# Sums of x moved from the matrix to the vector engine, scan products held over one step, two turns replaced by a transposing load

## The chip, the cores and the metric

The kernel runs on one core of one Trainium2 chip. The metric is the device time of one execution in microseconds (us), the median of several. For the experiments, five timed runs of each kernel were made in turns with nine of the kernel before on the same chip. The profiled execution gives a span that is about 2 us shorter than the time.

PE is the matrix engine (TensorE), PEld its weight loads, DVE the vector engine, ACT the scalar engine, POOL GpSimd, SP the sync engine that issues most DMAs.

## The reference, cut to what matters

Two independent parts on different inputs, put side by side in the output:

```python
# part A: a diagonal complex state space layer, T = 2048 tokens, D = P = 1024
Bu = einsum('bld,pd->blp', x, B_bar)
h[t] = Lam_bar * h[t-1] + Bu[t]                 # the scan
y = 2 * Re(einsum('blp,dp->bld', h, Cmat)) + x * Dskip
# part B: attention in 64 segments of 32 tokens, each with 8 memory rows that the segment before wrote
h = concat([mem, x_segment]); q, k, v = h @ Wq, h @ Wk, h @ Wv      # 32 heads of 128
o = softmax(mask(q k^T)) v @ Wo;  mem = o[:8]
```

The kernel first computes part A's scan (stage 1) together with part B's values v = x Wv, then part A's output (stage 2), then part B's attention and output. It breaks the chain of memories by a guess: the memory of a segment is guessed from the mean of its tokens (`xbar`), later checked. So it needs the sum of x over each segment of 32 tokens: the "sums of x".

## The kernel before

Stage 1 works in 32 steps, 8 groups of states by 4 blocks of 512 tokens. PE makes `u` (psU, two buffers), DVE turns it by a table, scans it, and turns it back (the "products" `n`, `h`); ACT makes `g`, a bf16 copy of the scan, between the two.

```python
def stage1(self, pc, tb):
    u = k.ps("U", (128, 2, TB))                  # 16 matmuls of 512 columns
    ...
    V.tensor_tensor(pr[:], u[:]..., t3, ALU.mult)            # a_pr<-psU: frees psU
    w = pr[:, :, 0, :]
    V.tensor_tensor(w, w, pr[:, :, 1, :], ALU.add)
    for j in range(2):
        V.tensor_tensor_scan(w[:, j, :], rb, w[:, j, :], ini, ALU.mult, ALU.add)
        S.activation(g[:, j, :], w[:, j, :], ACT.Copy)       # a_g, on the scalar engine
    ...
    V.tensor_tensor(n[:], g[:]..., r3, ALU.mult)             # a_n: has to wait for a_g
    V.tensor_tensor(h[:], n[:, :, 0, :], n[:, :, 1, :], ALU.add)
    k.SP.dma_start(self.hs[tb][:, pc, :, :], h[:])
```

Between the steps PE makes blocks of four value tiles into psP (three buffers), which ACT empties into `b_vst` in its own order:

```python
def v_x(self, hb, q, w):
    ...                                          # cut: the first block, below
    for i in range(4):
        p = k.ps("P")[:]
        self.v_mm(p, w, 4 * q + i)               # 8 matmuls of 512 columns
        k.copy("s", st[:, i, :, 0:E], p)         # b_vst<-psP on the scalar engine
    Q.dma_start(vx[...], st[...])
```

The sums of x are matmuls with a matrix of ones and zeros, on row tiles loaded for them alone; two tiles, that is 16 matmuls of 4 columns, stand before each of the scan steps 3 to 10. The first four token tiles are turned on PE:

```python
def sum_x(self, tmp):                            # cut
    p = k.ps("R")
    for t in range(TT):
        for c in range(KC):
            k.PE.matmul(p[:, o:o + 4], xr[:, c * 128:(c + 1) * 128], k.ind[:], start=True, stop=True)
        load(t + 4)

def turn_x0(self, i):                            # 8 transposes on PE, a copy on DVE or ACT
    for c in range(KC):
        k.PE.transpose(pt[:, c, :], self.x0[i][:, c * 128:(c + 1) * 128], k.ident[:])
    k.copy("vs"[i % 2], self.xe[:, :, 128 * i:128 * i + 128], pt)
```

Every instruction that `k.PE` issues is recorded at one helper line, L68; every copy at L93 (ACT) or L95 (DVE). Groups are told apart by the names of what they write and read.

## Time and profile before

| | before |
|---|---|
| time, median of 4 runs | 1243.44 us (1243.30 to 1243.81) |
| span of the profiled execution | 1241.5 us |
| PE busy | 1230.8 us, 99% |
| DVE busy | 667.8 us, 54%; but 53.5 of the 60 us from 100 to 160 us |
| PE's waits, all | 2.9 us in four |

From the page of the kernel before: engine busy time with its share of the span and the number of instructions recorded, the granted PE clock in tenths over 40 slices, and the chain of waits by engine.

```profile
PE 1230.8 (99%) x8246; PEld 658.8 (53%) x8318; DVE 667.8 (54%) x1254; ACT 266.6 (21%) x695; POOL 278.1 (22%) x442
PEclk9999999999999999999999999999999999999999
PE 96%; DMA 3%; issue 0%; SPq 0%; DVE 0%
```

PE is the whole story: it never stops and its clock is full. (Matmuls are pipelined: one of 512 columns is recorded with 379 ns, but the next starts 216 ns later. A wait that the list puts at 0.94 us therefore delays PE by 163 ns more, from start to start.) This is the full list of PE's waits of the kernel before: who waited for whom, us in total, how many times, the longest.

```profile
PE psR L68 <- DVE hpb L109: 1.3, 1, 1.3
PE psO L68 <- DMA b_v<-b_vx: 0.9, 1, 0.9
PE psP L68 <- DMA b_wv<-in_B_Wv_dram: 0.4, 1, 0.4
PE psU L68 <- DMA b_xr<-in_B_x_dram: 0.3, 1, 0.3
```

The chain of waits of the kernel before in order of time (start, length, what, how many instructions). It holds the landing of the first weights (at 2.85 + 6.71 us), the first `u`, one of eight bunches of sums, and two of the "values of the guess" (32 matmuls into psR), one in mid-stage and one at the end of stage 1.

```profile
2.85 6.71 DMA b_wv<-in_B_Wv_dram
...
36.57 3.45 PE psU L68 x16
...
67.65 0.38 PE psR L68 x16
...
171.00 0.93 PE psR L68 x32
...
347.40 0.93 PE psR L68 x32
```

The timeline of DVE of the kernel before, in two scan steps (start, length, line, operation, and in brackets the idle time before it with its releaser).

```profile
109.86 2.27 DVE L275 TENSOR_TENSOR a_pr<-psU,a_tabf 128x2048 f32<-128x2048 f32 x1
112.04 1.21 DVE L294 TENSOR_TENSOR a_n<-a_g,a_tabh 128x2048 bf16<-128x2048 bf16 x1
...
114.91 2.45 DVE L283 TENSOR_TENSOR_SCAN a_pr<-a_rr,a_nx,a_pr 128x512 f32<-128x512 f32 x2
118.05 1.23 DVE L294 TENSOR_TENSOR a_n<-a_g,a_tabh 128x2048 bf16<-128x2048 bf16 x1 [0.70 <-ACT a_g L284]
```

Two orders are to be seen. The first `a_n` here belongs to the step before and stands after the next `a_pr<-psU`: it waits for nothing. The last one comes right after its own scan and waits 0.70 us for `a_g`. DVE's waits in stage 1 (60 to 345 us) of the kernel before:

```profile
DVE a_n L294 <- ACT a_g L284: 15.3, 22, 0.7
DVE a_pr L275 <- PE psU L68: 10.1, 7, 2.0
```

So DVE is close to full from 100 to 160 us (53.5 of 60 us busy) but never holds PE.

### The profile page before, as it was taken

Reading aid. Unit: us, or ns where it says so; the run is one execution under the profiler, and the core shown is the slowest. Engines: PE = TensorE matmul, PEld = TensorE weight load, DVE = VectorE, ACT = ScalarE, POOL = GpSimd, SP = SyncE. Lnnn points to the kernel's source line nnn. Section 1 sums busy time; section 2 is a strip of 40 time slices with the busy share of each in tenths; the row PEclk is TensorE's granted clock in tenths of the full one; section 3 lists DMA queues with packets and bytes.
Section 4 is the critical chain, followed back from the end, with each engine's and each line's share of the span. In section 5 each row is a group of like instructions: output and inputs, shape, how many; then the busy total and the mean of one; then the engine's idle time right before and its main releaser. Section 6 shows DMA issues by size and latency. Waiting matters only on the chain.

```text
span 1241.5 us, 20294 instructions
## 1 busy us (share of the span) xinstructions
PE 1230.8 (99%) x8246; PEld 658.8 (53%) x8318; DVE 667.8 (54%) x1254; ACT 266.6 (21%) x695; POOL 278.1 (22%) x442
## 2 busy tenths in 40 slices
PE   9999999999999999999999999999999999999998
PEld 4444444444455555556565656556565654445444
DVE  4688899998811124666666666666666641001000
ACT  5344344443310000111112121212111210000000
POOL 4111331222322330232223232222322220000000
PEclk9999999999999999999999999999999999999999
DMA  9965444644898834675464554545564279507000
GB/s 251 267 184 158 131 120 133 156 143 118 221 325 247 267 109 106 150 200 139 109 153 108 126 135 114 131 94 140 112 146 101 59 198 252 113 17 154 17 17 27
DMA packets 322357, 178.42 MB, mean 144 GB/s; under 512 B 144666, under 2 KB 307660, under 8 KB 322260
## 3 DMA queue, kind: packets, MB, share of 16 engines
q1 hardware_dynamic: 300164, 149.53, 49.4%
q10 hardware_dynamic: 21072, 24.38, 6.0%
q0 software_dynamic: 1024, 3.17, 0.7%
q8 instruction: 66, 1.08, 0.4%
q14 instruction: 31, 0.25, 0.1%
HBM read 89.14 MB, written 53.96 MB: 115 GB/s over the span
## 4 chain that ended last, share of the span: by engine, by line
PE 96%; DMA 3%; issue 0%; SPq 0%; DVE 0%
PE psP L68 80%; PE psU L68 9%; PE psS L68 3%; PE psO L68 2%; DMA b_v<-b_vx 2%; PE psR L68 2%; DMA b_wv<-in_B_Wv_dram 1%; SPq L68 0%; DVE b_ost L95 0%; DVE b_vm L572 0%
## 5 line engine op out<-in xcount | busy, mean ns | idle before, releaser
L68 PE MATMUL psP<-b_xe,b_wq 128*128 128x480 bf16 (+1 forms) x1280 | 247.5, 343 | 0.1
L68 PE MATMUL psP<-b_xe,b_wk 128*128 128x480 bf16 (+1 forms) x1280 | 247.5, 343 | 0.0
L68 PE MATMUL psP<-b_wv,b_xe 128*128 128x512 bf16 (+2 forms) x1033 | 223.5, 372 | 1.2 <-DMA b_wv<-in_B_Wv_dram 0.4
L694 POOL TENSOR_TENSOR b_m<-b_e,maskB 99x396 bf16<-99x396 bf16 (+1 forms) x160 | 134.4, 840 | 337.0 <-ACT b_e L693 337.0
L693 ACT ACTIVATE b_e<-psS 99x396 bf16<-99x396 f32 (+3 forms) x208 | 91.3, 441 | 531.7 <-PE psS L68 523.4
L68 PEld LDWEIGHTS <-b_wk 128*128 128x128 bf16 x1280 | 119.2, 98 | 94.2
L68 PEld LDWEIGHTS <-b_xe 128*128 128x128 bf16 x1056 | 101.8, 98 | 119.6 <-issue 0.7
L68 PEld LDWEIGHTS <-b_wq 128*128 128x128 bf16 x1280 | 118.5, 98 | 87.7
L95 DVE CAST b_k<-psP 128x480 bf16<-128x480 f32 (+1 forms) x192 | 97.3, 528 | 100.9 <-PE psP L68 100.9
L95 DVE CAST b_q<-psP 128x480 bf16<-128x480 f32 (+1 forms) x192 | 97.3, 528 | 92.2 <-PE psP L68 90.9
L68 PEld LDWEIGHTS <-b_ol 128*128 128x128 bf16 x864 | 84.3, 98 | 94.4
L68 PE MATMUL psU<-a_xT,a_bt 128*128 128x512 bf16 x493 | 113.9, 379 | 1.1
L68 PE MATMUL psP<-t,a_hl 128*128 128x512 bf16 x496 | 112.1, 379 | 0.8
L95 DVE CAST b_ost<-psP 128x512 bf16<-128x512 f32 (+1 forms) x17 | 11.5, 676 | 177.6 <-PE psP L68 176.6
L68 PE MATMUL psP<-wo,b_ol 128*128 128x512 bf16 (+1 forms) x440 | 91.9, 364 | 0.4
L68 PE MATMUL psP<-t,b_ol 128*128 128x512 bf16 x408 | 91.7, 379 | 0.4
L288 POOL TENSOR_SCALAR a_tt<-a_pr,a_tabf 128x1 f32<-128x1 f32 x48 | 34.0, 709 | 242.6 <-DVE a_pr L283 242.6
L93 ACT ACTIVATE b_vst<-psP 128x512 bf16<-128x512 f32 x126 | 72.0, 588 | 72.4 <-PE psP L68 65.1
L711 DVE TENSOR_TENSOR b_ob<-psO,b_accR 99x384 bf16<-99x384 f32 x160 | 86.0, 554 | 2.2
L275 DVE TENSOR_TENSOR a_pr<-psU,a_tabf 128x2048 f32<-128x2048 f32 x32 | 73.0, 2282 | 16.2 <-PE psU L68 14.5
L68 PEld LDWEIGHTS <-a_bt 128*128 128x128 bf16 x512 | 49.2, 98 | 57.6
L68 PEld LDWEIGHTS <-a_hl 128*128 128x128 bf16 x512 | 49.0, 98 | 56.7
(204 smaller groups left out, 969.7 us busy)
## 6 DMA issues: line engine op xcount, KB each, us to landing
b_v<-b_vx SPq DMA_DIRECT2D x16, 1122.0 KB
b_wv<-in_B_Wv_dram SPq DMA_DIRECT2D x16, 1024.0 KB
b_vx<-b_vst ACTq DMA_DIRECT2D x24, 544.0 KB
b_on<-b_ob SPq DMA_DIRECT2D x15, 720.0 KB
a_hs<-a_h SPq DMA_DIRECT2D x32, 256.0 KB
b_wog<-in_B_Wo_dram SPq DMA_DIRECT2D x4, 2048.0 KB
b_wq<-in_B_Wq_dram SPq DMA_DIRECT2D x16, 512.0 KB
b_wk<-in_B_Wk_dram SPq DMA_DIRECT2D x16, 512.0 KB
```

What stands on the lines that cost most here:

```text
L68: r = f(*a, **kw)
L93: self.S.activation(out, in_, ACT.Copy)
L95: self.V.tensor_copy(out, in_)
L275: V.tensor_tensor(pr[:], u[:].unsqueeze(1).to_broadcast([128, 2, 2, TB]), view(t3, [[TB + 1, 2], [TB + 1, 2], [1, TB]]), ALU.mult)
L288: G.tensor_scalar(tt[:, j:j + 1], w[:, j, TB - 1:TB], t3[:, 1, TB:TB + 1], None, ALU.mult)
L693: k.S.activation(e[:, a:b, :, 0:n], s[0:GW, a:b, :, 0:n], ACT.Exp, scale=float(E) ** -0.5, accum_out=self.accE[0:GW, j:j + 1])
L694: k.G.tensor_tensor(mv[:, a:b, :, 0:n], e[:, a:b, :, 0:n], mask[0:GW, :, 0:n].unsqueeze(2).to_broadcast([GW, b - a, 2, n]), ALU.mult)
L711: V.tensor_tensor(self.ob[:, b0:b0 + n, :], o[0:GW, 0:n, 0:E], r.unsqueeze(2).to_broadcast([GW, n, E]), ALU.mult)
```

## The change

The intent: take the sums of x and two of the four turns off PE, which bounds the kernel; make room for the sums on DVE by holding each step's products until the next step's `a_pr<-psU` has been issued, so that they never wait for `a_g`. Two small things come with it: memory values of the first two head blocks are made two half tiles earlier in stage 2, and a transposing load in four pieces becomes one.

```diff
@@ stage1
+        self.form, last = None, self.form
         ...                                    # pr = u * table
+        if last is not None:
+            last()
         ...                                    # add, scans, a_g, carry
-        V.tensor_tensor(n[:], g[:]..., r3, ALU.mult)
-        V.tensor_tensor(h[:], n[:, :, 0, :], n[:, :, 1, :], ALU.add)
-        k.SP.dma_start(self.hs[tb][:, pc, :, :], h[:])
+        def form():
+            k.tc.keep_in_program_order(V.tensor_tensor(n[:], g[:]..., r3, ALU.mult))
+            V.tensor_tensor(h[:], n[:, :, 0, :], n[:, :, 1, :], ALU.add)
+            k.SP.dma_start(self.hs[tb][:, pc, :, :], h[:])
+        self.form = form
@@ sum_x
-        ... (row loads, 128 matmuls with k.ind)
+        for j in range(TT):
+            r = V.tensor_reduce(xs[:, :, 4 * j:4 * j + 4],
+                                self.xe[:, :, 128 * j:128 * j + 128].rearrange("p c (s t) -> p c s t", s=4), AX.X, ALU.add)
+            k.tc.keep_in_program_order(r)
+            yield
@@ first block of v_x
-            self.turn_x0(2)
             self.v_mm(ps[0], w, 0, 256, 512)
             self.v_mm(ps[1], w, 1, 256, 512)
-            self.turn_x0(3)
@@ v_mem
-            for h in range(4):
-                k.SP.dma_start_transpose(s[:, h, 0:E], self.vmt[hb][:, h * 128:(h + 1) * 128])
+            k.SP.dma_start_transpose(s[:, :, 0:E], self.vmt[hb][:])
@@ start
-            for i in range(4):
+            for i in range(2):
                 b.load_x0(p1, i)
-                if i in (1, 2):
-                    b.load_wv_part(w0, 0, 128 * i, (256, 512)[i - 1])
+            b.load_wv_part(w0, 0, 128, 256)
+            b.load_wv_part(w0, 0, 256, 512)
+            b.load_xp(64 + 256, 256, 256)       # transposing DMA
@@ loop of stage 1, step n
-                if n == 1:
-                    next(sx)
-                if n >= 3:
-                    for _ in range(2):
-                        next(sx, None)
                 a.stage1(pc, q)
+                for _ in range(2):
+                    next(sx, None)              # two reductions after each of steps 0 to 7
@@ loop of stage 2
-                if i in (26, 28):
+                if i in (24, 26):
                     vm = b.v_mem(...)
```

More of the change, by code (lines that the diff above doesn't have):

```diff
@@ L110, in consts @@
     k.S.activation(k.hpe[:], k.hpb[:], ACT.Exp)
-    k.ind = c.tile([128, 4], BF16, name="ind")
-    G.memset(k.ind[:], 0.0)
-    for j in range(4):
-        G.memset(k.ind[32 * j:32 * j + 32, j:j + 1], 1.0)
 def masks(k):
@@ L167, in __init__ @@
         self.Cre, self.Cim, self.logdt, self.Dskip, self.out = Cre, Cim, logdt, Dskip, out
+        self.form = None
         self.hs = [k.drp.tile([128, PC, 2, TB], BF16, name=f"a_hs{i}") for i in range(NB)]
@@ L291, in stage1 @@
             self.carry = nx
-        n = self.wp.tile([128, 2, 2, TB], BF16, name="a_n", bufs=1)
-        h = self.wp.tile([128, 2, TB], BF16, name="a_h", bufs=2)
-        V.tensor_tensor(n[:], g[:].unsqueeze(1).to_broadcast([128, 2, 2, TB]), view(r3, [[TB, 2], [TB, 2], [1, TB]]), ALU.mult)
-        V.tensor_tensor(h[:], n[:, :, 0, :], n[:, :, 1, :], ALU.add)
-        k.SP.dma_start(self.hs[tb][:, pc, :, :], h[:])
+        def form():
+            n = self.wp.tile([128, 2, 2, TB], BF16, name="a_n", bufs=1)
+            h = self.wp.tile([128, 2, TB], BF16, name="a_h", bufs=2)
+            k.tc.keep_in_program_order(
+                V.tensor_tensor(n[:], g[:].unsqueeze(1).to_broadcast([128, 2, 2, TB]), view(r3, [[TB, 2], [TB, 2], [1, TB]]), ALU.mult))
+            V.tensor_tensor(h[:], n[:, :, 0, :], n[:, :, 1, :], ALU.add)
+            k.SP.dma_start(self.hs[tb][:, pc, :, :], h[:])
+        self.form = form
     def s2_tiles(self, hpool, pool):
@@ L424, in sum_x @@
     def sum_x(self, tmp):
-        k = self.k
-        xrs = {}
-        def load(t):
-            if t < TT:
-                xrs[t] = tmp.tile([128, D], BF16, name="b_xr", bufs=4)
-                k.SP.dma_start(xrs[t][:], self.x[0][t * 128:(t + 1) * 128, :])
-        for t in range(4):
-            load(t)
-        yield
-        p = k.ps("R")
-        for t in range(TT):
-            xr = xrs.pop(t)
-            for c in range(KC):
-                o = c * NSEG + 4 * t
-                k.PE.matmul(p[:, o:o + 4], xr[:, c * 128:(c + 1) * 128], k.ind[:], start=True, stop=True)
-            load(t + 4)
+        k = self.k; V = k.V
+        xs = tmp.tile([128, KC, NSEG], FP32, name="b_xr", bufs=4)
+        for j in range(TT):
+            r = V.tensor_reduce(xs[:, :, 4 * j:4 * j + 4], self.xe[:, :, 128 * j:128 * j + 128].rearrange("p c (s t) -> p c s t", s=4),
+                                AX.X, ALU.add)
+            k.tc.keep_in_program_order(r)
             yield
-        pv = p[:].rearrange("p (c s) -> p c s", c=KC)
+        e = NSEG - 4
         ms = tmp.tile([128, KC], FP32, name="b_ms", bufs=1)
-        k.V.tensor_reduce(ms[:], self.m0T[:], AX.X, ALU.add)
-        k.V.tensor_scalar(self.xbar[:], pv, 1.0 / L, None, ALU.mult)
-        k.V.tensor_tensor(ms[:], ms[:], pv[:, :, 0], ALU.add)
-        k.V.tensor_scalar(self.xbar[:, :, 0], ms[:], 1.0 / L, None, ALU.mult)
+        V.tensor_reduce(ms[:], self.m0T[:], AX.X, ALU.add)
+        V.tensor_tensor(xs[:, :, e], xs[:, :, e], ms[:], ALU.add)
+        V.tensor_scalar(self.xbar[:, :, 2:NSEG - 2], xs[:, :, 0:e], 1.0 / L, None, ALU.mult)
+        V.tensor_scalar(self.xbar[:, :, 0:2], xs[:, :, e:e + 2], 1.0 / L, None, ALU.mult)
+        V.tensor_scalar(self.xbar[:, :, NSEG - 2:NSEG], xs[:, :, e + 2:NSEG], 1.0 / L, None, ALU.mult)
         yield
@@ L1100, in kernel_main @@
                     b.fill(p1)
+            a.form()
             k.pin.remove("PE")
@@ L1129, in kernel_main @@
                         pass
-                if i in (26, 28):
-                    vm = b.v_mem((i - 26) // 2, wv[(i - 26) // 2])
-                if 26 <= i < 30:
+                if i in (24, 26):
+                    vm = b.v_mem((i - 24) // 2, wv[(i - 24) // 2])
+                if 24 <= i < 28:
                     next(vm)
```

## The prediction

> What bounds it now. The matrix engine (PE) is busy 99% of the 1241.5 us span, the granted clock is full in every slice, and the chain of waits is 96% PE. The list of PE's waits holds only four: 1.3 us at the launch, 0.4 us for a part of the first value weights, 0.3 us for x, 0.9 us at 493 us for loaded value tiles (b_v<-b_vx). So time falls only where PE work or one of these waits goes; the vector engine (DVE, 54% overall) matters only where it begins to hold PE.
>
> Removed from PE, all on the chain of waits in order of time:
> - sums of x: eight bunches of 16 tiny matmuls at 0.38 us, 3.0 us;
> - two turns of x (16 transposes): one lies partly in the wait for weights, the other costs about 0.5 us. That weight part should also land about 0.7 us earlier.
> - the memory values of the first blocks come two half tiles (6.9 us) earlier, so the b_v load is issued earlier and the 0.9 us wait at 493 us should go.
>
> The price at the start: the third and fourth 128 tokens come by transposing DMA. In the trace's landings 1 MB so took about 6.5 us behind other traffic (160 to 230 KB/us; the Trainium skill, "DMA: Bandwidth & Descriptors", section on latency and other measured facts, gives 261 GB/s; the trace is below that). Half a megabyte after the weights (landed 9.56 us before, about 8.8 then) lands at 11 to 12.2 us by this estimate; PE would ask for it at about 10.6: a new wait of 0.5 to 1.5 us, which eats most of what the turns gave. Net at the start: 0 to 1 us gained.
>
> Added to DVE: 16 reductions of 1024 elements. The Trainium skill, "VectorE: DVE Perf Modes", section on the perf-mode tier table, lists reductions at 1x whatever the type; the trace's reductions of 704 and 208 elements (875 and 361 ns) agree and give about 1.21 us for 1024, so 19 us, in the first eight scan steps. (A strided one of 1120 took 2.16 us; this one reads runs of 32, so I expect the lower.) Given back: DVE waits 15.3 us in 22 waits of 0.7 us for the copies a_g on the scalar engine (list of DVE's waits, 60 to 345 us); held products hide these. A step then takes DVE about 7.5 us (as at 109.9 us, where the scheduler already interleaved so) plus 2.3 of reductions plus 0.8 of tables: 10.6, against PE's period of 10.36 us, and 3.45 where no value tile stands between. DVE falls up to 8 to 9 us behind near the eighth step. Two psU buffers just bear that, but the scalar engine's order puts a_g ahead of some evictions of value tiles (b_vst), and with three psP buffers I work out stalls of PE of 1 to 3 us in all between 105 and 160 us. After step 8 DVE has more room than before.
>
> Sum: -3.0 (sums), -0.9 (b_v wait), -0.5 (start), +2 (scalar engine holding psP): about -2.4 to -4. Predicted 1240.3 us, eight times in ten 1238.2 to 1243.3. Chances: faster by over 2% 0.5%, within 2% 99%, slower by over 2% 0.5%.
>
> What would show it: 144 matmuls fewer, PE's busy time some 3.5 us lower; reductions at 1.2 us; DVE's busy time up about 17 us, its a_g waits gone; a new PE wait for b_xe by DMA near 11 us; PE waits of psP for b_vst at 105 to 160 us; no b_v wait.
>
> What would make it wrong: reductions at 2 us (PE then held 5 us or more), a transposing load landing past 13 us, or no stall at all (then 1238).

## The result

| | before | changed |
|---|---|---|
| time, median of 4 runs | 1243.44 us | 1241.15 us (1241.03 to 1241.41) |
| span of the profiled execution | 1241.5 us | 1239.4 us |
| PE busy | 1230.8 us | 1227.3 us |
| DVE busy | 667.8 us | 676.2 us |

The ratio is 0.9981, 95% interval 0.9964 to 0.9999. (Ratios are computed as the mean time of one kernel's fast runs over that of the other's of the same rounds, so not quite the ratio of the medians quoted.) That is 2.3 us gained, within 2%.

The page of the changed kernel:

```profile
PE 1227.3 (99%) x8104; PEld 654.7 (53%) x8174; DVE 676.2 (55%) x1270; ACT 267.0 (22%) x694; POOL 268.7 (22%) x437
PE 93%; DVE 4%; DMA 2%; issue 1%; ACT 0%; another core or an unknown queue 0%; SPq 0%; DVEq 0%; ACTq 0%
```

PE lost 3.5 us of busy time and, by the weight loads, 144 matmuls (8318 - 8174). Both traces lack the records of some 70 matmuls (8246 and 8104 are recorded), about as many each, so the two busy times may be compared with each other, but not with those of runs whose records are complete (e2: 8174 matmuls, 1231.0 us). DVE appears in the chain that ended last with 4%, where it had nothing before. The list of PE's waits of the changed kernel:

```profile
PE psP L68 <- ACT b_vst L93: 2.3, 4, 0.9
PE psR L68 <- DVE hpb L109: 1.3, 1, 1.3
PE psU L68 <- DMA b_xr<-in_B_x_dram: 0.5, 1, 0.5
```

The waits for the first weights and for b_v are gone; four new ones, PE for a bank of psP that ACT had not emptied, have come. The same marks of the chain of waits in the changed kernel:

```profile
2.21 6.87 DMA b_wv<-in_B_Wv_dram
...
35.65 3.45 PE psU L68 x16
...
168.37 0.93 PE psR L68 x32
...
346.20 0.93 PE psR L68 x32
```

Laid beside those of before, the marks give a ledger. At the first `u` the changed kernel is 0.92 us ahead (36.57 - 35.65); this mark differs by some tenths from trace to trace, in the experiments that keep the new start it lies at 35.66 to 36.14. At the mark in mid-stage it is 2.63 ahead; at the end of stage 1 only 1.20, so 1.43 us were given back there. The values of the first attention pair, from the timelines, stand at 493.59 before (with the wait) and at 491.34 after: 2.25 ahead, so 1.05 us more gained in between.

```profile
493.59 0.50 PE L68 MATMUL psO<-b_v,b_m 128*128 128x129 bf16 x6 [0.88 <-DMA b_v<-b_vx]
```

```profile
491.34 0.50 PE L68 MATMUL psO<-b_v,b_m 128*128 128x129 bf16 x6
```

Where do the four waits stand? The first two, at 121.20 (0.94 us) and 131.95 us (0.24), lie in the last of the steps with reductions and just after it. The timeline of the changed kernel around the first:

```profile
118.85 0.63 ACT L284 ACTIVATE a_g<-a_pr 128x512 bf16<-128x512 f32 x1 [2.24 <-DVE a_pr L283]
119.39 0.71 ACT L238 ACTIVATE a_k<-a_tabf,a_bim 128x512 f32<-128x512 f32 x1
119.91 2.32 DVE L433 TENSOR_REDUCE b_xr<-b_xe 128x32 f32<-128x1024 bf16 x2
120.03 0.63 ACT L284 ACTIVATE a_g<-a_pr 128x512 bf16<-128x512 f32 x1
120.57 0.58 ACT L93 ACTIVATE b_vst<-psP 128x512 bf16<-128x512 f32 x1
121.20 1.89 PE L68 MATMUL psP<-b_wv,b_xe 128*128 128x512 bf16 x8 [0.94 <-ACT b_vst L93]
```

Read it upward. PE waits for a psP bank; ACT empties it at 120.57, the moment it is done with the two `a_g` (and a table copy) that stand before it in its order; `a_g` waited for the scan. DVE does not hold PE by its own buffer psU, but by way of ACT's order. The other two waits, at 336.79 (0.65 us) and 344.31 us (0.45), come at the end of stage 1, long after the last reduction:

```profile
334.45 0.63 ACT L284 ACTIVATE a_g<-a_pr 128x512 bf16<-128x512 f32 x1 [2.85 <-DVE a_pr L283]
335.62 0.63 ACT L284 ACTIVATE a_g<-a_pr 128x512 bf16<-128x512 f32 x1 [0.55 <-DVE a_pr L283]
336.16 1.55 ACT L93 ACTIVATE b_vst<-psP 128x512 bf16<-128x512 f32 x3
336.79 7.07 PE L68 MATMUL psP<-b_wv,b_xe 128*128 128x512 bf16 x31 [0.65 <-ACT b_vst L93]
343.66 1.57 ACT L93 ACTIVATE b_vst<-psP 128x512 bf16<-128x512 f32 x3 [4.35 <-DMA b_vx<-b_vst]
344.31 1.89 PE L68 MATMUL psP<-b_wv,b_xe 128*128 128x512 bf16 x8 [0.45 <-ACT b_vst L93]
```

For the wait at 336.79, ACT again stands at the last step's `a_g`, then empties three banks in a row. The wait at 344.31 ends differently: ACT had stood 4.35 us until a store of value tiles (`b_vx<-b_vst`) had landed and given its staging buffer free. The chain of waits has this store, from issue to landing:

```profile
331.62 11.96 DMA b_vx<-b_vst
```

The kernel before also waited there for a store (2.92 us of ACT, to 344.05), but PE, 1.8 us further back at this point, did not stand for it. At the place of the first of the two late waits the kernel before has another order on ACT, one eviction between the two `a_g`:

```profile
335.66 0.63 ACT L284 ACTIVATE a_g<-a_pr 128x512 bf16<-128x512 f32 x1 [3.17 <-DVE a_pr L283]
336.19 0.58 ACT L93 ACTIVATE b_vst<-psP 128x512 bf16<-128x512 f32 x1
336.83 0.63 ACT L284 ACTIVATE a_g<-a_pr 128x512 bf16<-128x512 f32 x1
```

What made that `a_g` late is the first question for the experiments. The reductions, and DVE's only wait from 60 to 345 us, in the changed kernel:

```profile
L433 DVE TENSOR_REDUCE b_xr<-b_xe 128x32 f32<-128x1024 bf16 x16 | 18.6, 1203 | 0.0
```

```profile
DVE a_pr L273 <- PE psU L68: 21.8, 11, 2.8
```

Reductions took 1.20 us each, and the waits for `a_g` are all gone from DVE's list.

### The profile page after: what moved, and what is told of

Its sections match the earlier page's. It is cut to its first block, busy times and chain, and to the rows that moved or that the text cites. A ratio compares the mean times of both kernels' runs of the same rounds, so it can differ in the third digit from the quotient of the medians.

```text
span 1239.4 us, 19975 instructions
## 1 busy us (share of the span) xinstructions
PE 1227.3 (99%) x8104; PEld 654.7 (53%) x8174; DVE 676.2 (55%) x1270; ACT 267.0 (22%) x694; POOL 268.7 (22%) x437
## 3 DMA queue, kind: packets, MB, share of 16 engines
q0 software_dynamic: 1024, 3.17, 0.8%
q8 instruction: 65, 1.06, 0.4%
## 4 chain that ended last, share of the span: by engine, by line
PE 93%; DVE 4%; DMA 2%; issue 1%; ACT 0%; another core or an unknown queue 0%; SPq 0%; DVEq 0%; ACTq 0%
PE psP L68 78%; PE psU L68 7%; PE psS L68 3%; PE psO L68 2%; PE psR L68 1%; DVE a_pr L283 1%; DVE a_pr L273 1%; DMA b_vx<-b_vst 1%; DVE b_xr L433 1%; DVE a_pr L278 1%; DMA b_wv<-in_B_Wv_dram 1%; ACT b_vst L93 0%; DVE a_h L298 0%; DVE a_tabh L239 0%
## 5 line engine op out<-in xcount | busy, mean ns | idle before, releaser
L288 POOL TENSOR_SCALAR a_tt<-a_pr,a_tabf 128x1 f32<-128x1 f32 x48 | 36.9, 768 | 251.0 <-DVE a_pr L283 251.0
L273 DVE TENSOR_TENSOR a_pr<-psU,a_tabf 128x2048 f32<-128x2048 f32 x32 | 73.0, 2282 | 26.4 <-PE psU L68 26.4
```

The source lines that it names most:

```text
L273: V.tensor_tensor(pr[:], u[:].unsqueeze(1).to_broadcast([128, 2, 2, TB]), view(t3, [[TB + 1, 2], [TB + 1, 2], [1, TB]]), ALU.mult)
L288: G.tensor_scalar(tt[:, j:j + 1], w[:, j, TB - 1:TB], t3[:, 1, TB:TB + 1], None, ALU.mult)
```

## The experiments

Theory: the two early waits come from the reductions, which make DVE late; the two late ones come from holding, because `n` and `h` of the step before now stand between `a_pr<-psU` and the scans; both reach PE through ACT's order and the three banks of psP. Rival 1: reductions cause all four. Rival 2: holding causes all four. Rival 3: DVE is simply short of throughput. Each edit below is against the changed kernel unless said otherwise. e1 to e4 ran on one chip, e5 to e8 on another, e9 to e11 on a third, e12 on a fourth, each with 9 runs of the kernel before (medians 1243.60, 1243.21, 1243.25 and 1243.30). All results were correct. The changed kernel itself was not run again on these chips, so what stands below as "over the changed kernel" compares different chips. Taken by way of the kernel before, which every chip ran, such differences shift by up to 0.4 us: e2 gains 1.35 us on the changed kernel (1.19 directly), e4 loses 3.8 (4.0), e5 1.12 (0.89), e6 1.29 (1.06). No conclusion hangs on that.

### e1: a fourth bank for value tiles

```diff
-                p = k.ps("P")[:]
+                p = k.ps("R" if i == 1 else "P")[:]
```

> The second value tile of every four goes to the psR bank, which is idle now that sums of x left it: four banks instead of three. Theory (the scalar engine stands at a_g and so does not empty psP): the four waits of PE for b_vst (2.3 us in the list of waits, 2.9 us from start to start of matmuls) go, 1238.3 us. Rival (the vector engine is short of throughput and holds PE in any case): the stalls move to psU and the time stays at 1241.2.

Measured: 1239.07 us (1238.87 to 1239.25), ratio to before 0.9963 (0.9950 to 0.9977). No wait for `b_vst` is left. The time is 0.8 us above the theory's. A new wait of 0.42 us stands at 173 us, where the psR bank still held values of the guess that DVE had not copied. So the stalls go through psP and ACT, not through psU: rival 3 falls. The change's own retreat from psR had left the bank that cures it.

### e2: the reductions elsewhere

```diff
             sx = b.sum_x(p1)
+            for _ in range(8):
+                next(sx)
...
-                for _ in range(2):
+                for _ in range(1):
                     next(sx, None)
```

> Same reductions, other places: eight in the vector engine's idle time before the first scan step, then one a step. Theory: the two early waits (near 121 and 132 us) come from reductions and go, 1.5 us, the two late ones (near 337 and 344 us) come from holding and stay: 1239.7 us. Rival 1 (reductions cause all four): 1238.3. Rival 2 (holding causes all four): 1241.2.

Measured: 1239.96 us (1239.83 to 1240.41). The early waits are gone and the late ones stand as they were (0.65 at 335.6 us, 0.48 at 343.2). The place of the reductions made the early two, and has no part in the late two. Rivals 1 and 2 both fail.

### e3: sums of x back on PE (spoiled by another wait)

`sum_x`, its loads, `k.ind` and the places of its matmuls as in the kernel before; the rest as changed.

> Sums of x back on PE as before, everything else of the change kept. Theory: 3.2 us of PE work come back, the two early waits (1.5 us) go, the two late ones (1.4 us) stay: 1242.9 us. Rival 1 (reductions cause all four): 1241.4 and no wait for b_vst. Rival 2 (holding causes all four): 1244.3.

Measured: 1251.38 us (1250.55 to 1252.38), 8.5 us over what the theory asked; the profiled execution was the slowest of the five, 9.5 us over. The timeline of e3 shows a thing that neither side had thought of:

```profile
49.84 0.63 ACT L238 ACTIVATE a_k<-a_fr 128x513 f32<-128x513 f32 x1 [13.39 <-DMA b_xe<-in_B_x_dram]
50.37 1.06 ACT L93 ACTIVATE b_vst<-psP 128x512 bf16<-128x512 f32 x2
51.00 3.57 PE L68 MATMUL psP<-b_wv,b_xe 128*128 128x512 bf16 x8 [6.56 <-ACT b_vst L93]
```

ACT stood 13.4 us before it issued a store of value tiles, until a load of x by SP had landed, and PE stood 6.6 us for a bank. The store does not use that x. In the built program it waits on a completion counter (DMAHW1) whose user before it is this load:

```
SP   14 DmaTransposeAnt b_xe<-in_B_x_dram 128x8x64 [waits DMAHW1_49]
ACT  39 DMACopy b_vx_68<-b_vst_169 128x4x544       [waits DMAHW1_49,Activation_49]
```

After its wait PE also ran at half clock. This is the window of e3 that follows it (window, length, busy time and count of PE, PEld, DVE, ACT and POOL, then the granted clock, DMA share and GB/s):

```profile
51.00:55.00 4.00, 4.00 (x10) 1.43 (x10) 0.00 (x0) 2.35 (x5) 0.00 (x0) 0.50 1.13 301
```

The clock records give 6.83 us at half speed, from 49.78 to 56.61. The Trainium skill, "TensorE: Matmul & The Clock Gate", Part 1, says that the matrix engine falls to half its clock after an idle window of about 3.4 us and returns after a busy one of that length; this trace agrees, and 6.83 us is about two windows of that length, an estimate from the page's figure. Wait and half clock together explain about 9.5 us (6.7 from start to start, 2.8 for 5.6 us at half speed after 51.00), all that the profiled execution took too long. The time says nothing clean of the theory, so the run was made again as e9; but its trace already shows what the theory asked, no early wait and the two late ones (0.65 at 348.1 us, 0.33 at 355.5).

### e9: as e3, one step later

```diff
-                if n == 1:          # of e3
+                if n == 2:
                     next(sx)
-                if n >= 3:
+                if n >= 4:
```

> As e3, with the row loads and the sums one scan step later, so that the store of value tiles which stood behind a transposing load of x in e3 (PE then waited 6.6 us at 51 us and ran 6.8 us at half its clock) shares its completion counter with an earlier load, as in the changed kernel. Theory: that wait goes, the two early waits of PE for b_vst (reductions) are gone, the two late ones (holding) stay at about 1.4 us, sums cost 3.2 us of PE: 1242.9 us. Rival 1 (reductions cause all four): 1241.4, no late waits. Rival 2 (holding causes all four): 1244.3, with waits at 105 to 160 us.

Measured: 1243.12 us (1243.03 to 1243.28). The long wait is gone. The full list of e9's waits for ACT:

```profile
PE psP L68 <- ACT b_vst L93: 1.1, 2, 0.7
```

Both are the late ones (0.65 at 338.7 us, 0.43 at 346.2). With the sums on PE and holding kept, the late waits stay: holding makes them. The 3.2 us of sums come back less the 1.5 us of early waits, as expected. The time is level with the kernel before (ratio 0.9999, 0.9986 to 1.0013), though e9 keeps the new start and the earlier memory values. Its marks show why: 0.74 us ahead at the first `u` (35.83), 0.67 behind at the end of stage 1 (348.07), 0.38 ahead at the first attention pair (493.21). The 1.41 us lost in stage 1 are the late waits.

### e4: products not held

`last()` and `a.form()` taken out, `form()` called at the end of its own step without its place being fixed.

> Products in their own step as before, sums on the vector engine. Theory: the late waits near 337 and 344 us go (1.4 us), but the vector engine waits 0.7 us for a_g again in each of the first steps and falls further behind, early waits of PE grow from 1.5 to 3 to 7 us: 1241.5 to 1246 us. Rival 1 (reductions cause all, holding is neutral): 1241.2 with late waits still there. Rival 2 (holding causes all four): 1238.3.

Measured: 1245.12 us (1244.92 to 1245.34), 1.5 us slower than before. The list of PE's waits in e4:

```profile
PE psP L68 <- ACT b_vst L93: 6.2, 3, 3.8
```

They stand at 113.7 (3.78 us), 160.5 (1.73) and 207.2 us (0.69); the late two are gone. Holding was needed for the sums where the change had put them, by 4.0 us net, and it makes the late waits.

### e8: neither held nor crowded

The reductions as in e2, the products as in e4.

> Reductions placed as in e2 and products not held at all. Theory: no cause of a stall is left except a little lateness in steps 4 to 8 where the vector engine has 10.7 us of work to PE's 10.36: 1238.3 to 1239.0 us. Rival 2 (holding is what makes the sums affordable): early waits of PE return, 1240 or more.

Measured: 1240.71 us (1240.09 to 1241.02). The theory's number fails: waits of 1.11 us at 111.2 us and 0.69 at 203.0 are left. So crowding is not the only cause of early waits; without holding DVE is late at 111.2 us even with one reduction a step, as rival 2 had said of this run. The wait at 203.0 (e4 has the same at 207.2) comes some 80 us after the last reduction, and what makes it was not traced. The five times fall in two groups, 1240.1 and 1240.7 to 1241.0, and the trace is of the upper group. Holding is worth about 1 us even with the reductions spread (e2 against e8: 0.75 directly, 1.14 by way of the kernel before), despite the 1.4 us that it costs late.

### e11: twice the reductions

Every `tensor_reduce` issued a second time; the result is unchanged.

> Every reduction twice (result unchanged): 18.6 us more of the vector engine in the first eight scan steps. Theory (the vector engine had no room left there: 10.6 us of work a step against PE's 10.36): nearly all of it reaches PE through the scalar engine's order, 1241.2 + 15 to 20 = 1256 to 1261 us, waits for b_vst between 60 and 160 us. Rival (the vector engine had room and the early waits are of another kind): under 1247.

Measured: 1253.32 us (1253.10 to 1253.51), 12.2 us over the changed kernel. The list of PE's waits in e11:

```profile
PE psP L68 <- ACT b_vst L93: 11.5, 7, 5.1
```

Second reductions of 19.2 us cost PE 12.2. About 2 us of that is the half clock again, by an estimate from the trace: it lasted 6.83 us after the 5.1 us wait, and PE worked for 4.0 of them. So the early steps have no room for more, as the theory says, but the expected 15 to 20 was too much: DVE's idle time before `a_pr` fell from 26.4 to 20.1 us (30 to 345 us), and those 6.3 us took up a third of the 19.2.

### e5, e6, e7: the small parts undone

e5 brings back the plain loads and turns of the third and fourth 128 tokens:

> Third and fourth 128 tokens again by plain loads and turns, all else of the change kept. Theory: the start loses what the trace shows it gained, 0.9 us: 1242.05 us, first block of value tiles ends at about 15.65 us. Rival (the later loads, which landed only 0.2 to 0.4 us ahead of PE, set the pace, so turns are free): 1241.2.

Measured: 1242.04 us (1241.87 to 1242.45), 0.89 over the changed kernel. The start's gain is real and about as large as the marks say.

e6 puts `v_mem` back to places 26 and 28:

> Memory values of the first blocks back at their old places, two half tiles later. Theory: PE's wait for b_v<-b_vx (0.9 us, 1.0 from start to start) returns: 1242.1 us. Rival (it went because of less DMA traffic or of the shorter stage before): no wait, 1241.2.

Measured: 1242.21 us (1241.94 to 1242.33), 1.06 over, with the wait for b_v<-b_vx back (0.85 us at 492.5 us). Moving the memory values is what removed it; the rival, less traffic or a shorter stage before, falls.

e7 splits the transposing load again:

> The transposing load of memory values in four pieces again. Theory: off the chain of waits, 1241.2 us within 0.2. Rival: one load instead of four freed the sync queue and part of the b_v gain is due to it: up to 1241.8.

Measured: 1240.98 us (1240.74 to 1241.24). No effect is seen.

### e10 and e12: causes taken away together

e10 is e2 with the fourth bank at the third tile (`i == 2`):

> e2's placing of the reductions with the psR bank as fourth, used for the third tile of four instead of the second, so that it is wanted 1.7 us later after the values of the guess (e1 waited 0.4 us there). Theory: no wait of PE for b_vst or b_ogT is left between 20 and 350 us: 1238.4 us, between 0.4 and 0.7 below e1. Rival: part of e1's rest is something else: 1239.0.

Measured: 1239.79 us (1239.46 to 1240.28). A miss: the values of the guess follow a block at once and now waited for that third tile to be emptied (0.55 and 0.37 us). e12 takes the second tile in such blocks and the third in others:

```diff
+                p = k.ps("R" if i == (1 if q == 3 else 2) else "P")[:]
```

> e10 with the psR bank for the second tile where values of the guess follow the block, and for the third otherwise, so that neither the eviction before them (0.55 and 0.37 us in e10) nor that of their result (0.42 us in e1) holds PE. Theory: no wait of PE for an eviction is left in the first 350 us, 0.9 to 1.2 us under e10 in the span: 1238.5 us, both kernels beaten. Rival: such waits only move to another bank: 1239 or more.

Measured: 1238.79 us (1238.44 to 1238.93), ratio to before 0.9963 (0.9950 to 0.9977), the lowest of all and 2.4 us below the changed kernel. Its list of PE's waits has no eviction of stage 1 left:

```profile
PE psR L68 <- DVE hpb L109: 1.3, 1, 1.3
PE psU L68 <- DMA b_xr<-in_B_x_dram: 0.5, 1, 0.5
PE psP L68 <- DMA b_wv<-in_B_Wv_dram: 0.3, 1, 0.3
PE psP L68 <- ACT b_xe L93: 0.2, 1, 0.2
```

Against e1 (1239.07, on another chip) the difference is within what chips and starts differ by: the spans are 1237.1 and 1237.2. Below the kernel before of their own chips they are 4.53 (e1) and 4.51 us (e12). The fourth bank gains as much alone; once it is there, no gain from spreading the reductions is shown.

## Why the prediction was right

The time was 1241.15 us, predicted 1240.3 with 1238.2 to 1243.3. The terms named were the right ones. That their sum came so near (-2.4 by the prediction's own terms, -2.3 measured) is in part luck: the gains were 0.8 us larger than predicted and the cost 0.9. Point by point:

| term | predicted | measured | how |
|---|---|---|---|
| sums of x off PE | -3.0 | -3.2 | marks: from 0.92 to 2.63 us ahead, plus the 1.5 lost to early waits between |
| start | -0.5 | -0.92 | marks; e5 gives 0.89 to 1.12 |
| b_v wait | -0.9 | -1.05 | marks; e6 gives 1.06 to 1.29 |
| ACT holding psP | +2 | +2.9 | 1.5 early (0.94 + 0.24 and 2 x 0.163), 1.43 late (marks) |
| sum | -2.4 to -4 | -2.3 (times), -2.1 (spans) | |

- The mechanism of the cost was named before it was seen: DVE late from the reductions, `a_g` late, ACT's order, psP. e1, e2 and e11 bear it out. The size of the part that was predicted, 1 to 3 us between 105 and 160 us, was right as well: 1.5 us. So was the lateness behind it, "up to 8 to 9 us behind near the eighth step": the eighth `u` was done at 104.7 us and DVE took it at 112.47, 7.8 us later (2.2 us in the kernel before, 107.6 to 109.86).
- What the prediction missed is the second half of that term. It held that "after step 8 DVE has more room than before". In throughput it has; but a step now takes longer from its `u` to its last `a_g`. At the end of stage 1 two `u` stand side by side, and from the start of the first one's `a_pr<-psU` to the end of the second one's last `a_g` it took 14.2 us before (323.26 to 337.46) and 15.6 us after (320.64 to 336.25), with `n` and `h` of the step before in between. e4 and e9 show that holding causes the late waits. The path goes with it in every trace: 14.2 us in the three kernels that do not hold (before, e4, e8), 15.6 in three that do (changed, e2, e9). But ACT's order goes with it too: in the three without holding an eviction stands between the last two `a_g`, in the three with it both `a_g` come first. An estimate from the changed kernel's trace: PE could have gone on at 335.98; with the eviction in its old place, between the two `a_g`, the bank would have been free at about 335.6 (334.45, plus 0.53 for the first `a_g`, plus 0.63 for the eviction), and the first late wait would not be. So it seems to take both, and no run separates them. The second late wait passes through the store that ACT issued at 331.62 and that landed 11.96 us later.
- The mis-sized term in the other direction is the start. The prediction asked for a new PE wait of 0.5 to 1.5 us for x by transposing DMA, and there is none: by the completion records of the trace the load landed at 10.73 us and its first matmul came at 11.08. The prediction had let the load begin when the weights ahead of it had landed, and had worked with 160 to 230 KB/us. But by the trace's packet records the load's 2048 packets of 256 bytes ran from 7.68 to 10.28 us; they began 1.4 us before the weights' landing (9.08 us). From 9 to 10 us, when they ran alone, 290 GB/s were moved. The Trainium skill, "DMA: Bandwidth & Descriptors", section on latency and other measured facts, gives 261 GB/s for one kernel with a non-contiguous middle dimension and about 350 to 400 for contiguous data; this load lies between. So the prediction's "the trace is below that" holds for landings alone: the transposing loads of the kernel before reach 290 GB/s too (33 to 35 us). The start has little room left: the second value weights landed at 14.60 us, 0.2 us before they were used, and in e12 PE did wait 0.32 us for them.
- The Trainium skill, "VectorE: DVE Perf Modes", section on the perf-mode tier table, lists reductions at 1x for bf16 and fp32 alike. The trace agrees: 1.203 us for 1024 bf16 elements, predicted 1.21 from two shorter fp32 reductions.
- "DVE's busy time up about 17 us" was wrong: it rose by 8.4 us. The reductions did add 18.6 us of busy time. But instructions of different steps, interleaved, overlap at their ends. Before, `a_n` at 112.04 us starts 0.09 us before the `a_pr` at 109.86 has ended (2.27 us), and held products have such neighbours in every step. Busy time counts an overlap once. Some copies left DVE too (one turn's, 0.69 us). Two runs bear it out: with the sums moved but nothing held (e4) DVE is busy 683.0 us, 15.2 more than before; with products held but the sums on PE (e9) it is busy 659.1, 8.7 less. So holding takes 7 to 9 us off DVE's busy time, which the prediction left out.

## What to carry to other kernels

Moving work from the engine that bounds a kernel to one that is "54% busy" costs what the stage allows, not what the whole span suggests: here DVE had nearly nothing left in the very steps that took the work, while it idled before the first of them. Look for the way a late engine reaches the bound one; it may be a third engine whose fixed order puts an urgent eviction behind a copy that is late. Then a further buffer can be worth more than a better place for the added work: here the fourth bank gained 2.1 us (e1) and the other places 1.2 (e2). And a reordering that removes waits on one engine may lengthen the path through a single step; check the places where steps stand back to back.

## What the Trainium skill lacked or had wrong

- "DMA: Bandwidth & Descriptors": the effective rate of transposing DMA is given as 261 GB/s or 350 to 400 for contiguous data. This case had 290 GB/s while such a load ran alone (9 to 10 us), and about 160 to 230 KB/us from landing to landing behind other traffic, an estimate. I found no page that says how much other traffic moves it.
- "TensorE: Matmul & The Clock Gate" says that an idle window of about 3.4 us halves the clock and that windows run freely. It is not wrong here; the runs add numbers: waits of 6.6 us (e3) and 5.1 us (e11) did so, for 6.83 us each time; a wait of 3.8 us (e4) did not.
- No page that I read says that a DMA issued by one engine may stand behind a load of another engine because the built program gave them the same completion counter. In e3 this held ACT 13.4 us and cost about 9.5 us of the profiled execution, the clock included; moving four loads by one step took it away (e9).
